# Chunked decay attention ahead of two feed-forward blocks: the work of two neighbouring chunks is issued together

## The chip, the cores and the metric

One Trainium2 chip, one of its cores. The metric is the device time of one execution in microseconds (us); lower is better. Engines are called as the profile calls them: PE (matmuls; PEld is its weight load), DVE (vector), ACT (scalar), POOL (GpSimd), SP (which issues the DMAs).

## What is computed

```
B, H, S, D = 2, 8, 768, 64
intra = (q k^T * decay_mask) v          # inside a block of tokens
inter = (q * lam^(pos+1)) state         # what earlier blocks left behind
out   = intra + inter
state = lam^block * state + (k * lam^(block-1-pos))^T v
x = relu(x w_in)^2 -> s*(.)+b -> w_out   # first feed-forward block
x = rms_norm(x); silu(x w_gate) * (x w_val) -> w_out   # second
```

The reference walks over blocks of 64 tokens, and the kernel over chunks of 128, which is the same recurrence. All is float32.

## The kernel before

There are NG = 12 chunks: 6 per batch row (NCH = 6), each with all 8 heads. Chunks are numbered g = 0 to 11, and c = g % 6 is the place in the batch row. Per chunk and in the names of the trace:

- **sc** (`scores`, L516): 8 matmuls k·q, 64 rows by 128 columns of the array each. DVE multiplies them with the decay into **prob** (L518), two instructions.
- **o** (L558): 8 matmuls v·prob, 128 rows by 64 columns. Then **qs** (L567): 4 matmuls state·qs, 128 by 128, into the same bank. `qs` itself is made by POOL (L530). For c = 0 there is no qs. ACT copies the bank into xq (L578, "the copy").
- **st** (L584): 8 matmuls kdec·v, 128 rows by 64 columns, the new state's part. **kdec** is made by ACT: 8 instructions of 128x64, one for each head (`prepare`, L535). For c = 5 there is neither kdec nor st.
- **state**: POOL scales the state of the chunk before (L546, `prepare_state`), DVE adds st to it (L597, `add_state`).

The order is written out by hand (`manual_schedule`): on every engine instructions run in the order in which the program text issues them. The loop at L624 issues, for chunk g: `prepare(g+1)`, `prepare_state(g)`, `outputs(g)` (o, qs, the copy, st), `add_state(g)`, `scores(g+2)`, then tasks of a table `plan`, which make the operands of the first feed-forward block on ACT and DVE (L143 and L146 split a value into two parts; L123, L129, L135, L140 turn raw words of the weights into numbers), then the loads of chunk g+4. At g = 11 two products of the first feed-forward block (**h**, L295) are issued ahead of `outputs(11)`. After it comes `spread_s`, a tiny matmul (L617) and a copy of its result by DVE (L618), which frees the bank that the third h product needs. Everything behind is one long row of matmuls of the two feed-forward blocks. The diff does not touch it.

Of the kernel before, what the change touches and what calls it, by code (L numbers as in the profile page):

```python
# [7 lines left out]
F32 = mybir.dt.float32  # L8
# [3 lines left out]
AF = mybir.ActivationFunctionType  # L12
# [3 lines left out]
P = 128  # L16
# [6 lines left out]
def attention_moe_moe2_kernel(  # L23
# [15 lines left out]
    nc = tc.nc  # L39
    NG, _, NPAIR, _ = qT.shape  # L40
    H = 2 * NPAIR
    D = P // 2
    B = 2
    NCH = NG // B
# [23 lines left out]
    def bank(i, name):  # L68
        return psum.tile([P, 512], F32, tag=f"b{i}", name=name)
# [5 lines left out]
    def piece(pool, tag, kbs, dtype=F32R):  # L75
        return pool.tile([P, int(kbs * KB)], dtype, tag=tag, name=f"{tag}_{len(made)}_{made.append(tag)}")
# [3 lines left out]
    def at(t, kb, kbs):  # L80
        return t[:, int(kb * KB) : int((kb + kbs) * KB)]
# [4 lines left out]
    def rows(ap):  # L86
        return ap.rearrange("p (k t) -> p k t", k=NK)
# [8 lines left out]
    m_g0 = piece(early, "g", 12, F32)  # L96
# [6 lines left out]
    xq = [rows(t) for t in m_q]  # L103
# [255 lines left out]
    def hquad(i):  # L359
        p, s_ = horder[i]  # L360
        if p < NPLAIN:
            yield from hplain(i)
            return
        ws, xs = w_set(p), ops1[s_]
        b0, b1, b2, b3 = hbanks(i)
        u2 = u2s[i % 2]
        product(b0, ws, xs, A11, B11)
        nc.scalar.activation(m_q1, b0, AF.Copy)
        while late_sq:
            r = late_sq.pop()  # L370
            nc.scalar.activation(r, r, AF.Square)
        yield
        product(b1, ws, xs, S2, T2)
        add(u2, b1, m_q1)
        yield
        r0, r1 = r_place(2 * p, s_), r_place(2 * p + 1, s_)
        u3 = r1[:, HB:BW]
        product(b2, ws, xs, S3, T3)
        add(u3, b2, u2)
        yield  # L380
        product(b3, ws, xs, S1, T1)

        add(u3, b3, u3)
        yield

        product(b0, ws, xs, A12, B21, True)
        nc.scalar.activation(r0[:, 0:HB], b0, AF.Relu)

        product(b2, ws, xs, A22, T4, True)
        add(r1[:, 0:HB], b2, u2)  # L390
        nc.scalar.activation(r1, r1, AF.Relu)

        product(b3, ws, xs, S4, B22, True)
        add(r0[:, HB:BW], b3, u2)
        nc.vector.tensor_scalar(r0[:, HB:BW], r0[:, HB:BW], 0.0, None, op0=ALU.max)
        nc.scalar.activation(r1, r1, AF.Square)
        late_sq.append(r0)
        yield
# [38 lines left out]
    with tc.tile_pool(name="att", bufs=1) as att:  # L437
        qt, kt, kvt = {}, {}, {}
# [14 lines left out]
        def load_chunk(g):  # L453
            if g < NG:
                load_qk(g)
                load_v(g)

        NPRE = 4
# [34 lines left out]
        for hf in range(2):  # L493
            pr = slice(hf * D, (hf + 1) * D)
# [10 lines left out]
        qs, prob, state, o_bank = {}, {}, {}, {}  # L505

        def scores(g):
            if g >= NG:
                return
            pt = att.tile([P, H, P], F32, tag="prob", bufs=3, name=f"prob{g}")  # L510

            sc = [bank(2 * (g % 2) + hf, f"sc{g}_{hf}") for hf in range(2)]
            for i in range(H):
                p, hf = divmod(i, 2)
                pr = slice(hf * D, (hf + 1) * D)
                nc.tensor.matmul(sc[hf][:, p * P : (p + 1) * P], kt[g][pr, p, :], qt[g][pr, p, :], start=True, stop=True)  # L516
            for hf in range(2):
                nc.vector.tensor_tensor(  # L518
                    pt.rearrange("p (a t) i -> p a t i", t=2)[:, :, hf, :],
                    sc[hf].rearrange("p (a i) -> p a i", i=P),  # L520
                    dec.rearrange("p (a t) i -> p a t i", t=2)[:, :, hf, :],
                    op=ALU.mult,
                )
            prob[g] = pt

        def prepare(g):
            c = g % NCH
            if c:
                t = att.tile([P, NPAIR, P], F32, tag="qs", bufs=2, name=f"qs{g}")
                nc.gpsimd.tensor_tensor(t, qt[g], lpow, op=ALU.mult)  # L530
                qs[g] = t
            if c < NCH - 1:
                kd = att.tile([P, H, D], F32, tag="kdec", bufs=2, name=f"kdec{g}")
                for h in range(H):
                    nc.scalar.activation(kd[:, h, :], kvt[g][:, 0, h, :], AF.Copy, scale=dec[:, h, P - 1 : P])  # L535
                qs[g, "kd"] = kd

        def prepare_state(g):
            c = g % NCH
            if c == NCH - 1:  # L540
                return
            sn = att.tile([P, NPAIR, P], F32, tag="state", bufs=2, name=f"state{g}")
            if c == 0:
                nc.gpsimd.memset(sn, 0.0)
            else:
                nc.gpsimd.tensor_tensor(  # L546
                    sn, state[g - 1], lpow[:, :, P - 1 : P].to_broadcast([P, NPAIR, P]), op=ALU.mult
                )
            state[g] = sn

        def outputs(g):
            c = g % NCH
            vn = kvt[g][:, 1]
            last = c == NCH - 1
            o = bank(4 + g % 2, f"o{g}")
            for h in range(H):
                pr = slice(h % 2 * D, (h % 2 + 1) * D)
                nc.tensor.matmul(  # L558
                    o[pr, h // 2 * P : (h // 2 + 1) * P],
                    vn[:, h, :],  # L560
                    prob[g][:, h, :],
                    start=h < 2,
                    stop=c == 0 and h >= H - 2,
                    skip_group_check=True,
                )
            for p in range(NPAIR if c else 0):
                nc.tensor.matmul(  # L567
                    o[:, p * P : (p + 1) * P],
                    state[g - 1][:, p],
                    qs[g][:, p],  # L570
                    start=False,
                    stop=p == NPAIR - 1,
                    skip_group_check=True,
                )
            o_bank[g] = o
            o3 = o.rearrange("p (a i) -> p a i", i=P)
            tok = slice(c * P, (c + 1) * P)
            nc.scalar.activation(xq[g // NCH][:, :, tok], o3, AF.Copy)  # L578
            if not last:
                kd = qs[g, "kd"]  # L580
                st = bank(6 + g % 2, f"st{g}")
                for h in range(H):
                    pr = slice(h % 2 * D, (h % 2 + 1) * D)
                    nc.tensor.matmul(  # L584
                        st[pr, h // 2 * D : (h // 2 + 1) * D], kd[:, h, :], vn[:, h, :], start=True, stop=True
                    )
                return st
            return None

        def add_state(g, st):  # L590
            if st is None:
                return
            st3 = st[:, 0 : NPAIR * D].rearrange("p (a i) -> p a i", i=D)
            sn = state[g]
            for hf in range(2):
                pr = slice(hf * D, (hf + 1) * D)
                nc.vector.tensor_tensor(sn[pr, :, pr], sn[pr, :, pr], st3[pr], op=ALU.add)  # L597

        scores(0)
        scan_lpow()  # L600
        scores(1)
# [9 lines left out]
        w0, w1 = (w_tasks(j, after_w(j)) for j in range(2))  # L611
# [9 lines left out]
            4: [xt["hB11"]], 5: [xt["lB11"], xt["hB21"]], 6: [xt["lB21"]] + w0[0:1], 7: [xt["hB12"]] + w0[1:2],  # L621
            8: [xt["lB12"]] + w0[2:4], 9: [xt["hB22"]] + w0[4:5], 10: [xt["lB22"]] + w1[0:1], 11: [spread_s],
        }
        for g in range(NG):  # L624
            if (g + 1) % NCH == 0 and g + 1 < NG:
                prepare_state(g + 1)
            if g + 1 < NG:
                prepare(g + 1)
            if g % NCH:
                prepare_state(g)  # L630
            if g == NG - 1:

                quad0 = hquad(0)
                next(quad0)
                next(quad0)
                for t in w1[1:]:
                    t()
            st = outputs(g)
            add_state(g, st)
            scores(g + 2)  # L640
            for t in plan.get(g, ()):
                t()
            load_chunk(g + NPRE)
            if g == 4:
                load_w(0, 0)
                load_w(0, 1)
            if g == 8:
                load_w(1, 0)
                load_w(1, 1)
                nc.sync.dma_start(g_col, rms_g.rearrange("(k p) -> p k", p=P))  # L650
                nc.sync.dma_start(row[:, H : H + 1], s.rearrange("(o h) -> o h", o=1))
                nc.sync.dma_start(row[:, H + 1 : H + 2], b.rearrange("(o h) -> o h", o=1))

    late = ctx.enter_context(tc.tile_pool(name="late", bufs=1))
    m_f.update({t: piece(late, t, kbs, F32) for t, kbs in (("u3", 28), ("u4", 15), ("u5", 15), ("u6", 4))})
# [133 lines left out]
    for blk in range(B):  # L789
# [46 lines left out]
        for it in range(by_f):  # L836
# [46 lines left out]
            if it in (3, 4):  # L883
                h = it - 3
# [175 lines left out]
    for i in range(len(order)):  # L1060
        for part, _ in enumerate(quad(i)):
            for t in plan.get((i, part), ()):
                t()
            f = (i + 3) // 2
# [121 lines left out]
```

## Time and profile before

| what | value |
|---|---|
| median of 3 runs | 594.76 us (594.65 to 594.83) |
| span of the profiled execution (first to last instruction) | 592.7 us |
| PE busy | 586.4 us, 99% of the span |
| ACT busy | 321.5 us, 54% |
| DVE busy | 407.8 us, 69% |
| POOL busy | 114.5 us, 19% |
| mean granted TensorE clock | 1.000 of full speed |
| kv load of a chunk, issue to landing | 6.3 us, median of 12 |

The profiled execution is told by its span alone; its own time around the span is not given. The median lies 2.06 us above the span (start and end of the program). Attention takes about the first 56 us of the span, and the rest belongs to the feed-forward blocks. In a timeline row stand the start, the length, the engine, the line, the operation, the tiles and how many instructions were merged; in square brackets stands the idle time of the engine before it and what ended it. Matmuls of float32 leave two records each, so 8 of them read x16.

### The profile page before, as it was taken

To read this page: it belongs to the slowest core of one execution; us is meant where nothing else is said; L and a number is where in the kernel's file an instruction comes from. 1 tells how busy PE (TensorE), PEld (TensorE's weight loads), DVE (VectorE), ACT (ScalarE), POOL (GpSimd) and SP (SyncE) were. 2 spreads that over 40 slices of the span, in tenths; PEclk is the share of its full clock that TensorE was granted. 3 is DMA by queue.
4 is the path that set the end of the run, shared out by engine and by line. 5 is a ranking of instruction groups with operands and counts; after the bars stand their busy time and mean duration, and the time that the engine had idled before them with its cause. 6 is when DMAs were issued, how large, how long until landed. Compare 5 with 4: busy or idle time off the path is not lost.

```text
span 592.7 us, 9212 instructions
## 1 busy us (share of the span) xinstructions
PE 586.4 (99%) x3590; PEld 543.1 (92%) x3590; DVE 407.8 (69%) x654; ACT 321.5 (54%) x572; POOL 114.5 (19%) x118
## 2 busy tenths in 40 slices
PE   9999999999999999999999999999999999999997
PEld 8888999999998888988888999999999998888886
DVE  6587957777777775769947986777777777874200
ACT  5677977777776663646542434444444445763200
POOL 3550032223103232041311002222222200000000
PEclk9999999999999999999999999999999999999999
DMA  8992202223223441221120001221222212320310
GB/s 312 334 350 72 72 1 78 77 72 131 72 72 110 139 143 35 71 69 38 36 72 1 1 2 71 72 72 71 72 72 71 86 58 77 136 72 1 142 38 35
DMA packets 17282, 51.98 MB, mean 88 GB/s; under 512 B 2390, under 2 KB 2390, under 8 KB 17238
## 3 DMA queue, kind: packets, MB, share of 16 engines
q1 hardware_dynamic: 17238, 51.39, 25.4%
q8 instruction: 28, 0.46, 0.3%
q14 instruction: 16, 0.13, 0.1%
HBM read 48.24 MB, written 3.15 MB: 87 GB/s over the span
## 4 chain that ended last, share of the span: by engine, by line
PE 93%; DVE 3%; ACT 2%; issue 1%; DVEq 0%
PE q L295 28%; PE h L295 17%; PE out L1078 17%; PE y L795 15%; PE z L807 8%; PE sc L516 2%; PE o L558 2%; PE o L567 2%; PE st L584 1%; PE warm L481 1%; PE rb L775 0%; DVE r_None L306 0%; PE nps L758 0%; DVE u_None L140 0%; ACT u_None L143 0%
## 5 line engine op out<-in xcount | busy, mean ns | idle before, releaser
L143 ACT ACTIVATE u_None<-u_None 128x768 fp32r<-128x768 f32 (+2 forms) x50 | 42.9, 871 | 55.0 <-DVE u_None L140 48.7
L295 PE MATMUL q<-u0b_None,u_None 128*128 128x384 f32 x360 | 68.4, 336 | 0.0
L295 PEld LDWEIGHTS q<-u0b_None,u_None 128*128 128x128 f32 x360 | 62.8, 188 | 0.6 <-DVE st_None L306 0.3
L146 DVE TENSOR_TENSOR u_None<-u_None,u_None 128x512 fp32r<-128x512 f32 (+1 forms) x66 | 54.1, 845 | 11.0 <-ACT u_None L143 11.0
L218 POOL TENSOR_TENSOR u_None<-u_None 128x256 f32<-128x256 f32 x18 | 19.9, 1103 | 188.6 <-DVE u_None L140 188.6
L295 PE MATMUL q<-xs_None,u_None 128*128 128x384 f32 x288 | 55.3, 334 | 0.0
L123 ACT ACTIVATE u_None<-st_None 128x512 f32<-128x512 f32 x68 | 45.2, 664 | 17.2 <-issue 14.3
L140 DVE CUSTOM_DVE_ANT_0 u_None<-u_None 128x1024 uint16<-128x1024 uint16 x68 | 47.8, 703 | 5.0
L295 PEld LDWEIGHTS q<-xs_None,u_None 128*128 128x128 f32 x288 | 50.4, 188 | 0.0
L129 ACT ACTIVATE u_None<-st_None 128x512 uint32<-128x512 uint16 x68 | 45.3, 666 | 5.1 <-DVE u_None L146 5.1
L306 DVE TENSOR_TENSOR st_None<-q,r_None 128x384 f32<-128x384 f32 x48 | 26.6, 553 | 18.8 <-PE q L295 18.7
L972 ACT ACTIVATE st_None<-r_None 128x384 f32<-128x384 f32 x24 | 12.6, 526 | 47.3 <-DVE r_None L306 47.3
L1078 PE MATMUL out<-u_None,xs_None 128*128 128x512 f32 x144 | 32.8, 389 | 0.0
L1078 PEld LDWEIGHTS out<-u_None,xs_None 128*128 128x128 f32 x144 | 27.0, 188 | 5.6
L1085 DVE COPY st_None<-out 128x512 f32<-128x512 f32 x4 | 2.8, 692 | 40.9 <-PE out L1078 40.9
L135 DVE TENSOR_SCALAR u_None<-u_None 128x512 uint32<-128x512 uint32 x68 | 30.1, 443 | 0.4
L424 POOL TENSOR_TENSOR wsum_None<-wsum_None,u_None 128x512 f32<-128x512 f32 x15 | 20.6, 1377 | 49.0 <-DVE u_None L140 49.0
L295 PE MATMUL q<-u0a_None,u_None 128*128 128x384 f32 x144 | 29.0, 335 | 0.2 <-DVE st_None L306 0.2
L295 PE MATMUL q<-g_None,u_None 128*128 128x384 f32 x144 | 26.9, 334 | 0.0
L295 PEld LDWEIGHTS q<-u0a_None,u_None 128*128 128x128 f32 x144 | 25.3, 188 | 0.5 <-DVE st_None L306 0.5
L1078 PE MATMUL out<-u_None,u0b_None 128*128 128x512 f32 x108 | 25.3, 389 | 0.0
L295 PEld LDWEIGHTS q<-g_None,u_None 128*128 128x128 f32 x144 | 25.1, 188 | 0.0
(202 smaller groups left out, 1310.4 us busy)
## 6 DMA issues: line engine op xcount, KB each, us to landing
st_None<-in_w_dram SPq DMA_DIRECT2D x68, 512.0 KB, 3.3
kv<-in_kv_dram SPq DMA_DIRECT2D x12, 512.0 KB, 6.3
q<-in_qT_dram SPq DMA_DIRECT2D x12, 256.0 KB, 6.8
k<-in_kT_dram SPq DMA_DIRECT2D x12, 256.0 KB, 6.5
out_dram<-st_None SPq DMA_DIRECT2D x8, 256.0 KB, 2.0
out_dram<-u_None SPq DMA_DIRECT2D x4, 256.0 KB, 2.1
row<-in_lam_dram SPq DMA_DIRECT2D x1, 0.0 KB
g_col<-in_rms_g_dram SPq DMA_DIRECT2D x1, 2.0 KB, 3.5
```

Source lines behind the costliest of these rows:

```text
L123: nc.scalar.activation(m, t[:, :, 1].bitcast(F32), AF.Prelu, scale=2.0**-112, alpha=-(2.0**32))
L129: nc.scalar.activation(to.bitcast(U32), low, AF.Copy, scale=2.0**-13)
L135: nc.vector.tensor_scalar(m, m, 3, None, op0=ALU.logical_shift_left)
L140: nc.vector.tensor_tensor(m, m, t.bitcast(U32), op=ALU.add)
L143: nc.scalar.activation(to, src, AF.Copy)
L146: nc.vector.tensor_tensor(to, src, hi.bitcast(F32), op=ALU.subtract)
L295: nc.tensor.matmul(ps, ws[:, wi, wop * KC + kt * P : wop * KC + (kt + 1) * P], xs[xop][:, xi, kt, :], start=n == 0 and not more, stop=n == ...
L306: nc.vector.tensor_tensor(to, ps, more, op=ALU.add)
L424: nc.gpsimd.tensor_tensor(wsum, wsum, m, op=ALU.add)
L795: nc.tensor.matmul(acc[d], wt[:, wi, d * P : (d + 1) * P], gt[:, gi, 0:BT], start=it == 0 and pi == 0, stop=it == NF1 - 1 and pi == 2,)
L807: nc.tensor.matmul(acc2[d // 2][:, d % 2 * BX : (d % 2 + 1) * BX], wt[:, wi, d * P : (d + 1) * P], gt[:, gi, BT:BW], start=it == 0 and pi ...
L1078: nc.tensor.matmul(ps, rows_[:, ai], w_out[f][:, wi, :], start=first and pi == 0, stop=last and pi == 2)
```

## The change

The loop goes over pairs of chunks. `outputs` is split into `states` (the st matmuls), `within` (the o matmuls) and `before` (the qs matmuls and the copy). For a pair g, g+1 it issues: st of both, o of both, `prepare_state(g)`, `add_state(g)`, qs and copy of g, `prepare_state(g+1)`, the tasks of g, `add_state(g+1)`, qs and copy of g+1, `prepare` of g+2 and g+3, sc of g+2 and g+3, the tasks of g+1, the loads of chunks g+4 and g+5. In the first pair o stands ahead of st. prob gets a fourth buffer, and the state moves to three places in a buffer that is otherwise unused at that time.

```diff
-            pt = att.tile([P, H, P], F32, tag="prob", bufs=3, name=f"prob{g}")
+            pt = att.tile([P, H, P], F32, tag="prob", bufs=4, name=f"prob{g}")
...
-            sn = att.tile([P, NPAIR, P], F32, tag="state", bufs=2, name=f"state{g}")
+            sn = at(m_g0, 2 * (g % 3), 2).rearrange("p (a i) -> p a i", i=P)
...
-        for g in range(NG):
-            if (g + 1) % NCH == 0 and g + 1 < NG:
-                prepare_state(g + 1)
-            if g + 1 < NG:
-                prepare(g + 1)
-            if g % NCH:
-                prepare_state(g)
...
-            st = outputs(g)
-            add_state(g, st)
-            scores(g + 2)
...
-            load_chunk(g + NPRE)
...
+        prepare(1)
+        for g in range(0, NG, 2):
+            if g:
+                st = [states(g + i) for i in range(2)]
+            within(g)
+            within(g + 1)
+            if not g:
+                st = [states(g + i) for i in range(2)]
+            if g % NCH:
+                prepare_state(g)
+            add_state(g, st[0])
+            before(g)
+            prepare_state(g + 1)
+            tasks(g)
+            if g + 2 == NG:
+                quad0 = hquad(0)
+                next(quad0)
+                next(quad0)
+                for t in w1[1:]:
+                    t()
+            add_state(g + 1, st[1])
+            before(g + 1)
+            for i in range(2, 4):
+                if g + i < NG:
+                    if (g + i) % NCH == 0:
+                        prepare_state(g + i)
+                    prepare(g + i)
+            scores(g + 2)
+            scores(g + 3)
+            tasks(g + 1)
+            for i in range(NPRE, NPRE + 2):
+                load_chunk(g + i)
+            fetch_more(g)
```

On PE, from the end of sc of chunk 3 on (the number behind a name's letters is the chunk; the last number is a buffer's). Before:

```order
L516 MATMUL sc3_1_281<-q3_111,k3_113 128x128
L558 MATMUL o2_311<-prob2_222,kv2_109 64x128 x8
L567 MATMUL o2_311<-qs2_241,state1_252 128x128 x4
L584 MATMUL st2_325<-kv2_109,kdec2_243 64x64 x8
L516 MATMUL sc4_0_337<-q4_235,k4_237 128x128
```

And now:

```order
L516 MATMUL sc3_1_284<-q3_111,k3_113 128x128
L558 MATMUL st2_307<-kv2_109,kdec2_249 64x64 x8
L558 MATMUL st3_316<-kv3_115,kdec3_260 64x64 x8
L568 MATMUL o2_325<-prob2_269,kv2_109 64x128 x8
L568 MATMUL o3_334<-prob3_282,kv3_115 64x128 x8
L581 MATMUL o2_325<-qs2_247,g_7_None_73 128x128 x4
L581 MATMUL o3_334<-qs3_258,g_7_None_73 128x128 x4
L516 MATMUL sc4_0_373<-q4_295,k4_297 128x128
```

The st matmuls moved from the end of a chunk's work to the front of the pair's, and each kind stands in one row for two chunks.

On ACT, where kdec is made and the outputs are copied, chunks 1 to 4. Before:

```order
L535 ACTIVATE kdec1_192<-kv1_103,dec_135 128x64 x8
L578 ACTIVATE xq0_5_None_71<-o0_201 128x4x128
L535 ACTIVATE kdec2_243<-kv2_109,dec_135 128x64 x8
L578 ACTIVATE xq0_5_None_71<-o1_254 128x4x128
L535 ACTIVATE kdec3_300<-kv3_115,dec_135 128x64 x8
L578 ACTIVATE xq0_5_None_71<-o2_311 128x4x128
```

And now:

```order
L535 ACTIVATE kdec1_191<-kv1_103,dec_135 128x64 x8
L590 ACTIVATE xq0_5_None_71<-o0_200 128x4x128
L590 ACTIVATE xq0_5_None_71<-o1_209 128x4x128
L535 ACTIVATE kdec2_249<-kv2_109,dec_135 128x64 x8
L535 ACTIVATE kdec3_260<-kv3_115,dec_135 128x64 x8
L590 ACTIVATE xq0_5_None_71<-o2_325 128x4x128
```

kdec of chunk g+1 stood ahead of the copy of chunk g; now kdec of both chunks of a pair stands behind both copies of the pair before.

Further on ACT, chunks 8 to 10 (L129 and L143 to u2 are tasks for the weights of the first h products), now:

```order
L590 ACTIVATE xq1_6_None_72<-o8_646 128x4x128
L129 ACTIVATE u1_2_None_68<-st0_11_None_77 128x512
L143 ACTIVATE u2_3_None_69<-u1_2_None_68 128x1024
L590 ACTIVATE xq1_6_None_72<-o9_655 128x4x128
L535 ACTIVATE kdec10_687<-kv10_620,dec_135 128x64 x8
```

Before, the copy of o9 stood behind kdec10; the two tasks already stood ahead of it.

## Rows read from the trace of the kernel before

**Rows 1.** Span and granted clock of the core; then the page's busy times.

```profile
core 0: 592.7 us, clock 1.000
...
PE 586.4 (99%) x3590; PEld 543.1 (92%) x3590; DVE 407.8 (69%) x654; ACT 321.5 (54%) x572; POOL 114.5 (19%) x118
```

**Rows 2.** Timeline of PE, one regular chunk: start, length, line, tiles, count.

```profile
15.18 1.16 PE L516 MATMUL sc<-q,k 64*128 64x128 f32 x16
16.27 1.09 PE L558 MATMUL o<-prob,kv 128*64 128x128 f32 x16
17.30 1.16 PE L567 MATMUL o<-qs,state 128*128 128x128 f32 x8
18.38 0.69 PE L584 MATMUL st<-kv,kdec 128*64 128x64 f32 x16
19.00 1.16 PE L516 MATMUL sc<-q,k 64*128 64x128 f32 x16
```

**Rows 3.** Timeline of PE, chunk 6, which has no qs.

```profile
30.93 1.09 PE L558 MATMUL o<-prob,kv 128*64 128x128 f32 x16
31.86 0.64 PE L584 MATMUL st<-kv,kdec 128*64 128x64 f32 x16
32.42 1.16 PE L516 MATMUL sc<-q,k 64*128 64x128 f32 x16
```

**Rows 4.** Timeline of PEld at two changes of tile shape.

```profile
17.29 0.97 PEld L567 LDWEIGHTS o<-qs,state 128*128 128x128 f32 x8 [0.17 <-issue]
...
53.10 0.85 PEld L558 LDWEIGHTS o<-prob,kv 128*64 128x64 f32 x16 [0.25 <-issue]
```

**Rows 5.** Timeline of ACT: kdec, copies, and the tasks of the plan.

```profile
12.84 2.01 ACT L535 ACTIVATE kdec<-kv,dec 128x64 f32<-128x64 f32 x8
14.75 0.58 ACT L578 ACTIVATE xq_None<-o 128x512 f32<-128x512 f32 x1
...
18.49 0.60 ACT L578 ACTIVATE xq_None<-o 128x512 f32<-128x512 f32 x1 [1.15 <-PE o L567]
...
26.62 0.84 ACT L143 ACTIVATE u0b_None<-xq_None 128x768 fp32r<-128x768 f32 x1
...
40.81 0.67 ACT L129 ACTIVATE u_None<-st_None 128x512 uint32<-128x512 uint16 x1
45.45 1.06 ACT L143 ACTIVATE u_None<-u_None 128x1024 fp32r<-128x1024 f32 x1 [3.98 <-DVE u_None L140]
46.42 2.01 ACT L535 ACTIVATE kdec<-kv,dec 128x64 f32<-128x64 f32 x8
```

**Rows 6.** Timeline of PE where that kdec is used, chunk 10.

```profile
47.39 1.42 PE L584 MATMUL st<-kv,kdec 128*64 128x64 f32 x16
48.73 2.35 PE L295 MATMUL h<-u0b_None,u_None 128*128 128x384 f32 x12
```

**Rows 7.** Timeline of PE: the first o, and the third h product.

```profile
9.78 1.19 PE L558 MATMUL o<-prob,kv 128*64 128x128 f32 x16
...
55.84 2.38 PE L295 MATMUL h<-u0b_None,u_None 128*128 128x384 f32 x12 [0.25 <-DVE params L618]
```

**Rows 8.** Timeline of DVE, first two chunks: prob of chunk 1, then the state.

```profile
11.27 0.68 DVE L518 TENSOR_TENSOR prob<-sc,dec 128x512 f32<-128x512 f32 x1
11.86 0.84 DVE L597 TENSOR_TENSOR state<-state,st 64x256 f32<-64x256 f32 x2
```

**Rows 9.** DVE's L140 at two places, and POOL beside the first.

```profile
43.88 1.54 DVE L140 CUSTOM_DVE_ANT_0 u_None<-u_None 128x1024 uint16<-128x1024 uint16 x1
...
51.29 0.69 DVE L140 CUSTOM_DVE_ANT_0 u_None<-u_None 128x1024 uint16<-128x1024 uint16 x1
...
43.42 1.45 POOL L530 TENSOR_TENSOR qs<-q,lpow 128x512 f32<-128x512 f32 x1 [1.10 <-PE o L567]
```

**Rows 10.** ACT's copy of o10, and the end of the chain of tasks on DVE.

```profile
49.54 0.58 ACT L578 ACTIVATE xq_None<-o 128x512 f32<-128x512 f32 x1
...
55.63 0.16 DVE L618 COPY params<-params 128x2 f32<-128x2 f32 x1
```

More of the change, by code (lines that the diff above doesn't have):

```diff
@@ L549, in prepare_state, with states, within @@
             state[g] = sn
-        def outputs(g):
-            c = g % NCH
+        def states(g):
+            if g % NCH == NCH - 1:
+                return None
+            vn, kd = kvt[g][:, 1], qs[g, "kd"]
+            st = bank(6 + g % 2, f"st{g}")
+            for h in range(H):
+                pr = slice(h % 2 * D, (h % 2 + 1) * D)
+                nc.tensor.matmul(
+                    st[pr, h // 2 * D : (h // 2 + 1) * D], kd[:, h, :], vn[:, h, :], start=True, stop=True
+                )
+            return st
+        def within(g):
             vn = kvt[g][:, 1]
-            last = c == NCH - 1
             o = bank(4 + g % 2, f"o{g}")
@@ L562, in outputs, with before @@
                     start=h < 2,
-                    stop=c == 0 and h >= H - 2,
+                    stop=g % NCH == 0 and h >= H - 2,
                     skip_group_check=True,
                 )
+            o_bank[g] = o
+        def before(g):
+            c, o = g % NCH, o_bank[g]
             for p in range(NPAIR if c else 0):
@@ L574, in outputs @@
                 )
-            o_bank[g] = o
-            o3 = o.rearrange("p (a i) -> p a i", i=P)
             tok = slice(c * P, (c + 1) * P)
[L578 to L588, printed above, removed]
+            nc.scalar.activation(xq[g // NCH][:, :, tok], o.rearrange("p (a i) -> p a i", i=P), AF.Copy)
         def add_state(g, st):
@@ L623, in attention_moe_moe2_kernel, with tasks, fetch_more @@
         }
-        for g in range(NG):
-            if (g + 1) % NCH == 0 and g + 1 < NG:
-                prepare_state(g + 1)
-            if g + 1 < NG:
-                prepare(g + 1)
-            if g % NCH:
-                prepare_state(g)
[L631 to L637, printed above, removed]
-            st = outputs(g)
-            add_state(g, st)
-            scores(g + 2)
+        def tasks(g):
             for t in plan.get(g, ()):
                 t()
-            load_chunk(g + NPRE)
+        def fetch_more(g):
             if g == 4:
```

## The prediction

> **What bounds the kernel now.** I read the page first: PE is busy 586.4 of the 592.7 us of the span, and ACT half of it [rows 1]. So PE's own time is the limit, and a change pays only where it shortens that time and does not make PE wait. Next I read PE's timeline through attention. A regular chunk is sc 1.09, o 1.03, qs 1.08, st 0.62, from start to start, 3.82 us in all, with no gap [rows 2]. The next thing to see is that part of this is paid for changing kinds. In chunk 6, which has no qs between o and st, the two take 1.49 instead of 1.03 + 0.62 = 1.65 [rows 3]: one change of tile shape less, 0.16 us less. PEld's timeline shows the same thing from the other side, a gap of 0.17 to 0.25 us that nothing releases at each change [rows 4]. I take 0.20 us for a change, between 0.16 and 0.25. Last I read ACT, because the order shows that its instructions move. There kdec takes 1.91 us to the next start, and 0.10 of an instruction's length overlaps the next one, so a copy costs 0.48 [rows 5].
>
> The place that decides my forecast is one that went wrong already before the change. From 41.5 to 45.45 ACT stood still for 3.98 us in front of a task (L143) that waited for DVE; kdec of chunk 10 stood behind it and began only at 46.42 [rows 5]. On PE st of chunk 10 then took 1.42 instead of 0.69, and h began at 48.73, which is 0.30 after kdec's end at 48.43 [rows 6]. So ACT takes its instructions in order, and PE waits in st for a late kdec, with everything behind it. 0.20 of the 0.30 is the change of shape, so 0.10 is the handover, which I use for every handover below.
>
> **What the change takes away.** Counted from the first o to the third h product (9.78 to 55.84 us [rows 7]) PE changes shape 42 times before. With the change it does so 18 times, because st and o have one shape and stand together, and qs of chunk 10, h and qs of chunk 11 do too. That is 24 changes less: 24 x 0.20 = **4.8 us less** (3.8 to 6.0). A pair that never waits would take 7.64 - 5 x 0.20 = 6.64 us.
>
> **What it adds.** kdec of a pair now stands on ACT behind both copies of the pair before it, and the last copy waits for the last qs on PE. But st of the new pair is what PE wants right after sc. Let S be the start of sc of a pair. The copy starts 0.11 after PE has left qs, as at 18.38 and 18.49 [rows 2, 5]. Then the first o can start at 0.11 + 0.48 + 2 x 1.91 + 0.10 + 0.10 = S + 4.61. Without the wait it would be sc twice, 2 x 1.09 - 0.20 = 1.98, and st twice, 2 x 0.42, so S + 2.82. PE waits 1.79 us. Then o twice, 2 x 1.03 - 0.20 = 1.86, and qs twice, 2 x 1.08 - 0.20 = 1.96. **A pair lasts 8.43 us where it lasted 7.64.** The five changes saved are there, and the wait eats more.
>
> The whole path on PE, pair by pair:
> - Pair 0, 1: o of chunk 1 waits for its prob, which ends at 11.27 + 0.68 = 11.95 [rows 8]; before, sc of chunk 2 stood in that time. Handover 0.10, seven of eight heads 0.73, st of chunk 0 0.42, handover 0.10, `add_state` 0.84 [rows 8], handover 0.10, qs 1.08: sc of chunk 2 starts at 15.3.
> - Pair 2, 3: 8.43, to 23.8.
> - Pair 4, 5: chunk 5 has no kdec. 0.11 + 0.48 + 1.91 + 0.20 = 2.70, o 1.86, qs 1.96: 6.52, to 30.3.
> - Pair 6, 7: the task hB11 (L143, 0.74) stands between the two copies of chunks 4 and 5. The first copy starts at S - 0.97 and ends at S - 0.49, the task ends at S + 0.25, the second copy at S + 0.73. kdec twice and handover 4.02, o 1.86, and only one qs, 1.08: 7.69, to 38.0.
> - Pair 8, 9: the copy of chunk 6 needs no qs and is early, so the two word tasks between the copies (2 x 0.57) are over in time: 8.43, to 46.4.
> - Pair 10, 11: after the copy of chunk 8 (S - 0.49) come L129 (0.57), L140 on DVE, L143 (0.97), the copy of chunk 9 (0.48), then one kdec with its handover 2.11, o 1.86, qs of chunk 10 without a change 0.88. L140 takes 0.69 us alone and took 1.54 while POOL made a qs [rows 9]; in the new order POOL makes two qs just there, so I take 1.54. Sum 7.92, and h starts at 54.3 (53.5 with 0.69). It was 48.73.
> - The third h product needs the copy L618, behind the tasks of ACT and DVE that begin with the copy of chunk 10: 49.54 to 55.84 took 6.30 [rows 7, 10]. PE itself needs 7.11 - 1.03 = 6.08, as o of chunk 11 is done earlier. So 0.11 + 6.30 after h: 60.7.
>
> 60.7 against 55.84 is **+4.9 us**: 4.8 gained, 9.7 given to waits. Behind this point the same matmuls follow in the same order, at 99% [rows 1], and the loads of weights come no later against PE, so I carry the 4.9 to the end. The sum stands on one profiled execution with a span of 592.7 [rows 1]; the span becomes 597.6, and the median, 2.06 us above the span, 594.76 + 4.9 = **599.7 us**.
>
> What I cost at nothing: the state's chain (POOL scales, DVE adds, 1.9 us for a chunk) is needed only one pair later for the first chunk, and after o twice for the second; if it were late, qs would wait. The added DVE distance between prob and its o is covered by the kdec wait itself. The loads of chunks g + 4 and g + 5 are let go later: the kv buffer for chunk 6 is free when o of chunk 2 is done, near 15.3 + 5.5 = 20.8, and kdec wants chunk 6 near 30.3 + 0.7 = 31.0. That is 10 us, and a kv load landed in 6.3 us (the table of the profile before). The state's new place costs nothing to anyone.
>
> The Trainium skill, TensorEngine Tiling (Array Packing), PSUM Bottleneck, says that after a speedup by tiling the copies out of PSUM may become the limit. Here the rows weigh otherwise. DVE reads four prob and two `add_state` pairs for a pair of chunks, 4 x 0.68 + 2 x 0.84 = 4.4 us [rows 8], and ACT's copies take 0.96, both below 6.64. By that rule alone nothing would bind and the sum would be -4.8; by the rows it is +4.9, since kdec and not a copy is late.
>
> **Unknown sizes.** The 1.54 may be 0.69: 4.0 instead of 4.9. A change of 0.25 or 0.16 instead of 0.20 moves some nine pieces that are on the path by 0.05 or 0.04: -0.45 or +0.36. Handovers may be 0.2 instead of 0.1, two or three for a pair: up to +1.3. So the forecast's own range is +3.3 to +6.7, 598.0 to 601.5.
>
> **Rivals.**
> - *Only the changes of shape count (faster).* If kdec is ready when sc ends, because the copies are early or ACT runs kdec quicker, PE never waits and the time is 594.76 - 4.8 = 590.0. For it: 24 changes really go. Against it: 3.8 us of kdec do not fit beside 2 us of sc, and the order has them behind the copies. The point that decides: a pair of chunks breaks even with 7.64 when one kdec takes 1.91 - 0.79 / 2 = 1.52 us. Chance 6%. The Trainium skill, TensorEngine Tiling (Array Packing), Key Properties, says that changing the tiling mode drains the TensorE; by that rule alone this rival would be right, and the trace's 0.16 agrees on the drain.
> - *The two cancel.* If the first pair and the last one cost less than written (5.5 and 7.9 us), and pairs break even, the time is within 0.2% (1.2 us), which is about what a measurement of this kernel can tell from no change: 594.8. For it: two of six pairs have one kdec or none late. Against it: pair 2, 3, pair 6, 7 and pair 8, 9 each lose 0.8 us or more. Chance 5%.
> - *The waits also slow PE's clock (slower still).* The granted clock is 1.000, the level of 2.4 GHz, with PE at 99% [rows 1]; now PE stands still for 1.8 us in each of several pairs. At 1.2 GHz one pair would need 5.6 to the first o, then 3.72 and 3.92: 13.2 instead of 8.43, so +4.8 and 604.5 for one pair. Against it: the st at 47.39 held a wait of 0.73 us, and 12 h records after it took 2.35 us as against 2.38 later [rows 6, 7]. Chance 4%. The Trainium skill, TensorE: Matmul & The Clock Gate, Part 1, says that the clock is throttled unless activity releases it; no trace here shows how short a wait is harmless.
>
> **How the numbers follow.** The forecast, waits for kdec beyond the gain, has 85%, and gives 599.7. Faster 6%, same 5%, slower 89% (85 and 4). The range leaves out the faster rival, most of "cancel" and the clock, some 15%, and is a little wider than the forecast's own: 597.5 to 602.5.
>
> **What would show it.** In the profile after: PE's st of the second chunk of pairs 2, 3, 6, 7 and 8, 9 some 1.8 us long, or idle there with ACT kdec as releaser; sc, sc, st, o of a pair from S to S + 8.4; h at 54 and its third product near 60.7; L140 near 46.5 long beside POOL. It is wrong if sc of chunk 4 starts before 22.5 (15.3 + 7.2), or if ACT's kdec of chunk 2 starts before the copy of chunk 1, or if PE busy falls by 5 us and the span with it.

## The result, and the profile after

| | before | with the change |
|---|---|---|
| median | 594.77 us | 600.62 us (600.47 to 601.08, 4 runs) |
| ratio | | 1.0104, 95% interval 1.0092 to 1.0116 |
| span of the profiled execution | 592.7 us | 598.5 us |

The kernel is 1% slower, 5.85 us; forecast were 599.7 (597.5 to 602.5) and slower. The page after shows where not to look:

```profile
PE 589.6 (99%) x3590; PEld 546.9 (91%) x3590; DVE 409.4 (68%) x654; ACT 321.9 (54%) x572; POOL 114.5 (19%) x118
```

PE's busy time did not fall by 4.8 us, it rose by 3.2 [rows 1]: the st matmuls trickle in, one for each kdec instruction every 0.24 us, and their records are 0.22 to 0.27 us long, so the wait between them counts as busy. So the waits are read from starts. PE's timeline after, the starts of all pairs from chunk 2 on (st and o of two chunks read x32, or x31 beside a stray row of one; `g_None` is the state's new place):

```profile
15.72 2.06 PE L516 MATMUL sc<-q,k 64*128 64x128 f32 x32
17.70 2.87 PE L558 MATMUL st<-kv,kdec 128*64 128x64 f32 x31
...
20.47 1.91 PE L568 MATMUL o<-prob,kv 128*64 128x128 f32 x31
22.31 2.05 PE L581 MATMUL o<-qs,g_None 128*128 128x128 f32 x16
24.29 2.06 PE L516 MATMUL sc<-q,k 64*128 64x128 f32 x32
...
31.02 2.06 PE L516 MATMUL sc<-q,k 64*128 64x128 f32 x32
...
39.02 2.06 PE L516 MATMUL sc<-q,k 64*128 64x128 f32 x32
...
47.59 2.06 PE L516 MATMUL sc<-q,k 64*128 64x128 f32 x32
50.55 1.94 PE L558 MATMUL st<-kv,kdec 128*64 128x64 f32 x15 [0.90 <-ACT kdec L535]
...
55.14 2.35 PE L295 MATMUL h<-u0b_None,u_None 128*128 128x384 f32 x12
...
61.70 2.35 PE L295 MATMUL h<-u0b_None,u_None 128*128 128x384 f32 x12 [0.92 <-DVE params L620]
```

st of chunks 2 and 3 takes 2.77 us to the next group, where the same 16 matmuls without a wait take 0.98 (the kernel with kdec early, below). All the other kinds go at the pace the sum used. The third h product starts at 61.70 instead of 55.84 [rows 7], 5.86 us later, and the span is 5.8 us longer: behind it nothing came back and nothing was added. ACT's timeline after, ahead of pair 2, 3 and of the last pair:

```profile
15.82 0.60 ACT L590 ACTIVATE xq_None<-o 128x512 f32<-128x512 f32 x1 [3.43 <-PE o L581]
16.32 3.93 ACT L535 ACTIVATE kdec<-kv,dec 128x64 f32<-128x64 f32 x16
...
46.80 0.60 ACT L590 ACTIVATE xq_None<-o 128x512 f32<-128x512 f32 x1 [1.88 <-PE o L581]
47.30 0.66 ACT L129 ACTIVATE u_None<-st_None 128x512 uint32<-128x512 uint16 x1
48.72 1.06 ACT L143 ACTIVATE u_None<-u_None 128x1024 fp32r<-128x1024 f32 x1 [0.76 <-DVE u_None L140]
49.68 0.58 ACT L590 ACTIVATE xq_None<-o 128x512 f32<-128x512 f32 x1
50.16 2.01 ACT L535 ACTIVATE kdec<-kv,dec 128x64 f32<-128x64 f32 x8
```

ACT stands idle for 3.43 us in front of a copy that waits for qs, with kdec of chunks 2 and 3 queued behind it; then PE waits for kdec, which ends at 20.25, and o follows at 20.47. At the end of the stage the two tasks and the copy of chunk 9 stand between, and kdec of chunk 10 starts only at 50.16, 2.57 us after sc.

### The profile page after: what moved, and what is told of

It is laid out like the page before. It is cut to its first block, busy times and chain, and to the rows that moved or that the text cites. A ratio compares the mean times of both kernels' runs of the same rounds, so it can differ in the third digit from the quotient of the medians.

```text
span 598.5 us, 9209 instructions
## 1 busy us (share of the span) xinstructions
PE 589.6 (99%) x3590; PEld 546.9 (91%) x3590; DVE 409.4 (68%) x654; ACT 321.9 (54%) x572; POOL 114.5 (19%) x118
## 4 chain that ended last, share of the span: by engine, by line
PE 92%; DVE 3%; ACT 3%; issue 1%; DVEq 0%; ACTq 0%
PE q L295 28%; PE out L1101 16%; PE h L295 16%; PE y L818 15%; PE z L830 8%; PE st L558 2%; PE sc L516 2%; PE o L568 2%; PE o L581 2%; PE warm L481 1%; PE rb L798 0%; DVE u_None L140 0%; DVE r_None L306 0%; PE nps L781 0%; ACT u_None L123 0%
## 5 line engine op out<-in xcount | busy, mean ns | idle before, releaser
L143 ACT ACTIVATE u_None<-u_None 128x768 fp32r<-128x768 f32 (+2 forms) x50 | 42.8, 870 | 51.8 <-DVE u_None L140 45.5
L140 DVE CUSTOM_DVE_ANT_0 u_None<-u_None 128x1024 uint16<-128x1024 uint16 x68 | 47.0, 691 | 6.0 <-ACT u_None L129 1.2
L129 ACT ACTIVATE u_None<-st_None 128x512 uint32<-128x512 uint16 x68 | 45.2, 665 | 5.1 <-DVE u_None L146 5.1
L135 DVE TENSOR_SCALAR u_None<-u_None 128x512 uint32<-128x512 uint32 x68 | 31.0, 455 | 2.0 <-ACT u_None L123 1.6
L295 PE MATMUL h<-u0b_None,u_None 128*128 128x384 f32 x126 | 24.3, 337 | 0.9 <-DVE params L620 0.9
```

Source lines behind the costliest of these rows:

```text
L129: nc.scalar.activation(to.bitcast(U32), low, AF.Copy, scale=2.0**-13)
L135: nc.vector.tensor_scalar(m, m, 3, None, op0=ALU.logical_shift_left)
L140: nc.vector.tensor_tensor(m, m, t.bitcast(U32), op=ALU.add)
L143: nc.scalar.activation(to, src, AF.Copy)
L295: nc.tensor.matmul(ps, ws[:, wi, wop * KC + kt * P : wop * KC + (kt + 1) * P], xs[xop][:, xi, kt, :], start=n == 0 and not more, stop=n == ...
```

## The experiments

Theory A: kdec stands on ACT behind the copies, st stands on PE at the front of a pair, and the two together make the wait. Rival B: the pairs as such cost, by prob, the state or the loads, and kdec only hides it. The fourth prob buffer and the state's new place stand in every version of the change below.

**kdec early.** `prepare` is split, and its kdec part is issued as soon as st has freed the buffers:

```diff
...
+            for i in range(2, 4):
+                if g + i < NG:
+                    prepare_k(g + i)
             if g % NCH:
                 prepare_state(g)
             add_state(g, st[0])
             before(g)
```

> The change with one thing undone: kdec of the next pair is issued on ACT ahead of both copies of this pair (st and o have just freed its buffers). Theory A (PE waits in st because kdec stands behind the copies): st of a pair no longer waits, a pair lasts 6.6 to 6.9 us instead of 8.57, h starts near 48.8 instead of 55.1, and the time falls by 6 to 7 us, to 594.3 (593.5 to 595). Rival B (the pairs themselves cost: prob, the state's chain or the loads are late and kdec only hides it): another wait takes the place, a pair stays at 8 us or more and the time at 599 or above.

Measured 596.79 us, ratio 1.0026 (1.0012 to 1.0039). PE's timeline of this kernel:

```profile
15.72 2.06 PE L516 MATMUL sc<-q,k 64*128 64x128 f32 x32
17.70 1.15 PE L561 MATMUL st<-kv,kdec 128*64 128x64 f32 x32
18.68 1.92 PE L571 MATMUL o<-prob,kv 128*64 128x128 f32 x32
20.53 2.05 PE L584 MATMUL o<-qs,g_None 128*128 128x128 f32 x16
22.51 2.06 PE L516 MATMUL sc<-q,k 64*128 64x128 f32 x32
...
29.25 2.06 PE L516 MATMUL sc<-q,k 64*128 64x128 f32 x32
...
35.77 2.06 PE L516 MATMUL sc<-q,k 64*128 64x128 f32 x32
...
38.74 2.29 PE L571 MATMUL o<-prob,kv 128*64 128x128 f32 x32
...
43.05 2.06 PE L516 MATMUL sc<-q,k 64*128 64x128 f32 x32
...
47.45 4.07 PE L571 MATMUL o<-prob,kv 128*64 128x128 f32 x32 [1.73 <-DVE prob L518]
51.45 1.16 PE L584 MATMUL o<-qs,g_None 128*128 128x128 f32 x8
52.36 2.33 PE L295 MATMUL h<-u0b_None,u_None 128*128 128x384 f32 x12
```

In pair 2, 3 theory A holds: 8.57 became 6.79, near the 6.64 of a pair that never waits. Pair 8, 9 went from 8.57 to 7.28 only, as o took 2.22 instead of 1.85 to the next group, and pair 4, 5 stayed (6.74 after 6.73). The time fell by 3.8 us and not by 6 to 7. The last pair took 9.31 from sc to h instead of 7.55. There rival B has its part: o of chunk 10 waits 1.73 us for prob, and DVE is why.

```profile
42.75 1.27 DVE L135 TENSOR_SCALAR u_None<-u_None 128x512 uint32<-128x512 uint32 x1
44.16 1.54 DVE L140 CUSTOM_DVE_ANT_0 u_None<-u_None 128x1024 uint16<-128x1024 uint16 x1
45.73 0.85 DVE L602 TENSOR_TENSOR g_None<-g_None,st 64x256 f32<-64x256 f32 x2
46.61 2.48 DVE L518 TENSOR_TENSOR prob<-sc,dec 128x512 f32<-128x512 f32 x4
```

The words of the first weights stand ahead of prob of chunk 10, and both DVE instructions are stretched (0.42 and 0.69 us elsewhere in the trace). The late kdec had covered that. And o behind the wait takes twice its time (4.07 instead of 1.92). The windows of this execution (their length, then the busy time of PE, PEld, DVE, ACT and POOL, then the granted clock and what the DMAs did) say why:

```profile
46.00:48.00 2.00, 0.45 (x4) 0.24 (x4) 1.96 (x5) 2.00 (x3) 1.84 (x2) 0.96 0.15 11
48.00:50.00 2.00, 2.00 (x20) 2.00 (x22) 2.00 (x4) 0.01 (x1) 0.00 (x0) 0.50 0.00 0
50.00:52.00 2.00, 2.00 (x19) 1.78 (x15) 1.96 (x4) 0.00 (x0) 0.00 (x0) 0.68 0.00 0
```

PE was busy for 0.45 of 2 us, and then the clock was granted at half, 1.2 GHz, until some time after 50. That loses some 0.04 x 2 + 0.50 x 2 + 0.32 x 2 = 1.7 us, an estimate from these rows. Half of this kernel's six executions had a mean clock of 0.996 and took 597.4 to 597.6, the others 595.7 to 596.2: at the full clock, too, it is slower than the kernel before (595.04 in this round).

**kdec late in the old order.** The kernel before, with kdec of chunk g+1 moved behind the copy of chunk g:

```diff
...
             st = outputs(g)
+            if g + 1 < NG:
+                prepare_k(g + 1)
```

> The kernel before with kdec of chunk g+1 moved behind the copy of chunk g, and nothing else. Theory A says that the place behind the copy hurts only together with st at the front: here st of chunk g+1 comes 3.82 us after st of chunk g and kdec is done 0.11 + 0.48 + 1.91 + 0.20 = 2.70 us after it, so nothing waits in the regular chunks; 594.8 to 595.6, a little only at chunk 10, where tasks stand in between. Rival B2 (kdec behind the copy costs wherever st stands): about 0.8 us for each of nine chunks, 600 or more.

Measured 595.39 us, ratio 1.0002 (0.9993 to 1.0012). In the regular chunks nothing waits, though kdec now starts right behind the copy; st keeps its 0.69, and sc of two neighbouring chunks stand 3.82 apart (15.09 and 18.91) as before:

```profile
14.58 0.60 ACT L581 ACTIVATE xq_None<-o 128x512 f32<-128x512 f32 x1 [1.16 <-PE o L570]
15.07 2.01 ACT L538 ACTIVATE kdec<-kv,dec 128x64 f32<-128x64 f32 x8
18.29 0.69 PE L587 MATMUL st<-kv,kdec 128*64 128x64 f32 x16
```

So kdec behind the copy is harmless as long as sc, o and qs of the next chunk stand ahead of the st that wants it; at chunk 10, with the tasks between, st took 1.90 instead of 1.42. It takes both halves of the change, as theory A has it.

**st behind o.** All pairs with `within` ahead of `states`, as the first has it.

> The change with st of both chunks behind o of both in every pair, as the first pair has it. kdec stays behind the copies. Theory A: o twice (1.66 us) moves into the wait for kdec, so each pair with two kdec gains 1.1 to 1.7 us, up to what the state (DVE's add behind st, ahead of qs) gives back; 597.0 (596 to 598.5). Rival B (not kdec but the pairs as such): no gain, 600.6.

Measured 601.03 us, ratio 1.0103 (1.0086 to 1.012): a miss. Three pairs did gain from sc to sc (2, 3: 7.66 us instead of 8.57; 6, 7: 7.45 instead of 8.00; 8, 9: 8.09 instead of 8.57), but pair 4, 5 lost (7.47 instead of 6.73): o right behind sc waits for DVE's four prob, and o twice took 2.46 there instead of 1.85. The last pair lost too: sc of chunk 10 to h took 8.30 instead of 7.55, with PE standing in front of o of chunk 10 (PE, then DVE):

```profile
49.70 2.72 PE L568 MATMUL o<-prob,kv 128*64 128x128 f32 x31 [2.10 <-ACT xq_None L590]
...
48.91 2.48 DVE L518 TENSOR_TENSOR prob<-sc,dec 128x512 f32<-128x512 f32 x4
```

The profile names ACT's copy of o9 as what ended the wait. But by the program that copy empties the bank of o of chunk 11; the bank of o of chunk 10 had been copied out by 45.4. What o of chunk 10 needs is its prob, which begins on DVE only at 48.91, behind the two word tasks, as in kdec early; its halves end at 49.60 and 50.20, and the first two heads of o start at 49.70 and 50.25. Three of the four executions had a mean clock of 0.996 or 0.997 and took 600.5 to 601.5; the profiled one had the full clock and took 599.26, which is above the expected range as well. I had costed the matmuls that move into the wait, and not the prob that they need.

**kdec in half the instructions.**

```diff
-                for h in range(H):
-                    nc.scalar.activation(kd[:, h, :], kvt[g][:, 0, h, :], AF.Copy, scale=dec[:, h, P - 1 : P])
+                for h in range(0, H, 2):
+                    nc.scalar.activation(kd[:, h : h + 2, :], kvt[g][:, 0, h : h + 2, :], AF.Copy, scale=dec[:, h, P - 1 : P])
```

> The change with kdec in 4 ACT instructions of 128x128 for a chunk instead of 8 of 128x64; the second head of each two gets the decay of the first, which leaves out part of the computation. One kdec takes about 1.15 us instead of 1.91, which is under the 1.52 us at which a pair breaks even with the kernel before. Theory A: 2 x 0.75 us less for each pair with two kdec and 0.75 for those with one, as far as the wait reaches: 594.6 (594 to 596). Rival B: 600 or more.

Measured 596.88 us, ratio 1.0033 (1.0024 to 1.0043): 3.7 us less than the change, its order untouched, and above the expected 594 to 596. Pair 2, 3 lasts 7.09 (15.71 to 22.80) instead of 8.57. So the dose matters, which rival B cannot explain. The point of breaking even was right for a pair (7.09 is below 7.64), and wrong for the whole, as the first and last pairs carry waits of another kind: sc of chunk 10 (43.32) to h (51.70) took 8.38 instead of 7.55, with kdec of chunk 10 behind a word task that waited for DVE.

```profile
47.90 1.21 PE L558 MATMUL st<-kv,kdec 128*64 128x64 f32 x16 [2.52 <-ACT kdec L535]
```

**The price of a change of shape.** kdec early, but with qs of the first chunk between the two o:

```diff
...
             within(g)
-            within(g + 1)
+            if g % NCH == 0:
+                within(g + 1)
...
             before(g)
+            if g % NCH:
+                within(g + 1)
```

> kdec early, but in pairs 2, 3, 4, 5, 8, 9 and 10, 11 qs of the first chunk stands between the two o, as in the kernel before: two more changes of tile shape in a pair, same matmuls. If a change costs 0.16 to 0.25 us, the pairs 2, 3 and 4, 5 last 0.3 to 0.5 us longer than with kdec early alone (6.79 and 6.74 us), less what the later second o saves by waiting less for its prob (at most 0.3 in pair 4, 5). If a change costs nothing on the path, they last the same 6.8.

Measured 596.07 us, ratio 1.0031 (1.0021 to 1.0041). Pair 2, 3 of this kernel:

```profile
15.71 2.06 PE L516 MATMUL sc<-q,k 64*128 64x128 f32 x32
17.70 1.15 PE L561 MATMUL st<-kv,kdec 128*64 128x64 f32 x32
18.68 1.09 PE L571 MATMUL o<-prob,kv 128*64 128x128 f32 x16
19.70 1.16 PE L584 MATMUL o<-qs,g_None 128*128 128x128 f32 x8
20.78 1.09 PE L571 MATMUL o<-prob,kv 128*64 128x128 f32 x16
21.81 1.16 PE L584 MATMUL o<-qs,g_None 128*128 128x128 f32 x8
22.90 2.06 PE L516 MATMUL sc<-q,k 64*128 64x128 f32 x32
```

It lasts 7.19 us with two changes more, against 6.79: 0.20 us for each. In pairs 4, 5 and 8, 9 the two cost next to nothing (6.75 against 6.74, 7.27 against 7.28), since the later o no longer waits for its prob. The whole kernel was not slower than kdec early either (596.07 and 596.79; at the full clock 595.5 to 596.1 and 595.7 to 596.2). The gain is real, and it counts only where nothing else is late.

**Repairs, one behind the other.** First the words go behind prob of chunks 10 and 11, then the tiny matmul of `spread_s` gets another bank, one that sc used, then the first two chunks go back to nearly the old order, last the words go between the two prob:

```diff
...
-            8: [xt["lB12"]] + w0[2:4], 9: [xt["hB22"]] + w0[4:5],
+            8: [xt["lB12"]], 9: w0[2:4] + w0[4:5] + [xt["hB22"]],
...
-            pps = bank(6, "params2")
+            pps = bank(3, "params2")
```

> kdec early, and the word tasks of the first weights (L129, L135, L140, L143) moved from the tasks of chunk 8 to those of chunk 9, which is behind prob of chunks 10 and 11 on DVE and behind kdec and both copies on ACT. Theory C (with kdec early the last pair waits because DVE's prob stands behind that chain of words: 9.31 us from sc of chunk 10 to h): o of chunk 10 no longer waits for prob, PE's long wait near 46 us goes and with it the half clock behind it; sc of chunk 10 to h takes 6.5 to 7.5 us, some of which the first h product gives back by waiting for its words; 595.0 (594 to 596). Rival D (the words are late whatever stands ahead of them): the wait moves to h unchanged, 596.5 to 597.

595.79 us, ratio 1.0014 (1.0005 to 1.0024), no half clock in the stage. sc of chunk 10 to h took 6.42 instead of 9.31. The first h product gave 1.0 of it back, waiting for DVE's words (3.20 to the next product instead of 2.17), and the third waited 1.38 instead of 0.94. Theory C holds for the wait in front of o and for the clock; the rest of the wait moved on, as rival D has it. Against the kernel before of its own round (594.82) this version is 0.97 us slower; the executions of kdec early at the full clock were 0.7 to 1.2 slower than theirs. So the repair took away the half clock and little else.

> The same, and the tiny matmul of spread_s writes to a bank that sc used, so the third h product no longer waits for DVE's copy L620. Expected where the copy is what it waits for: the wait of 0.93 us ahead of the third h product goes, 0.9 to 1.6 us less than the kernel without this, 593.8 (593 to 595), which would be below the kernel before. Where the second weights' words are what counts, the wait moves to the fifth product and nothing is gained.

594.53 us, ratio 0.9993 (0.9983 to 1.0002): the wait ahead of the third h product is gone, the time equal to the kernel before.

> Control: the kernel before with the tiny matmul of spread_s on another bank, and nothing else. Only the wait of 0.25 us ahead of the third h product can go: 594.5 to 594.8, the same within what can be told. If it gains 0.9 us or more, the gain of the bank has nothing to do with the pairs.

594.16 us, ratio 0.9988 (0.9979 to 0.9998), 0.37 below the repaired pairs of the same round: so far pairing gains nothing over the old order with the same bank. Beside the last two kernels once more:

> The control once more, beside the two: the kernel before with the other bank. 594.2, the same as before (594.0 to 594.6).

594.74 us, ratio 0.9997 (0.9988 to 1.0006). Both medians of the control lie just outside what was expected of them, one below and one above; they are 0.58 us apart, so a gain of that size can't be told here. The bank alone is worth at most that in the old order, where o of chunk 11 stands ahead.

> As the version with kdec early, words behind prob and the other bank, but chunks 0 and 1 in nearly the old order: o and st of chunk 0, sc of chunk 2, o and st of chunk 1, qs of chunk 1, sc of chunk 3; pairs from chunk 2 on. Theory E (pairing pays for the changes saved with waits where nothing else stands between dependent steps, 2.15 us of them in the first pair): sc of chunk 2 covers the wait for prob of chunk 1, st of chunk 2 starts 1.2 to 1.4 us earlier against the first o, two changes more; 593.3 (592.8 to 594), faster than the kernel before by 0.2 to 0.3%. Rival: the wait comes back later at the loads or the words, and the time stays at 594.5.

```diff
+        within(0)
+        add_state(0, states(0))
+        before(0)
...
+        scores(2)
+        within(1)
+        add_state(1, states(1))
...
+        before(1)
...
+        scores(3)
...
+        for g in range(2, NG, 2):
```

593.47 us, ratio 0.9981 (0.9972 to 0.999): 1.06 us less than without it (measured in another round), 1.27 less than the control of the same round (594.74), which is about twice what the control's two medians differ by, and 0.2% below the kernel before. The fourth prob buffer and the state's new place are in it, so they do not make the loss. sc of chunk 2 now covers the wait for prob of chunk 1:

```profile
10.99 1.16 PE L516 MATMUL sc<-q,k 64*128 64x128 f32 x16
12.08 1.09 PE L571 MATMUL o<-prob,kv 128*64 128x128 f32 x16
13.01 0.63 PE L561 MATMUL st<-kv,kdec 128*64 128x64 f32 x16
13.57 1.16 PE L584 MATMUL o<-qs,g_None 128*128 128x128 f32 x8
14.66 1.16 PE L516 MATMUL sc<-q,k 64*128 64x128 f32 x16
```

> The same, with the words of the first weights between prob of chunk 10 and prob of chunk 11 on DVE instead of behind both. The first h product no longer waits 1.3 us for its words, o of chunk 11 waits up to 1 us more for its prob: between 0.5 us less and nothing, 592.8 to 593.5.

594.71 us, ratio 0.9998 (0.9989 to 1.0006): a miss. o of chunk 11 waited 1.56 us for its prob, and in the profiled execution the clock went to half behind it. That is not all: the ten executions with a mean clock of 0.999 or 1.000 have a median of 594.5. The wait was moved to a worse place.

## Why the prediction was right, point by point

| step, from sc to sc | forecast | measured |
|---|---|---|
| first pair, to sc of chunk 2 | 15.3 | 15.72 |
| pair 2, 3 | 8.43 | 8.57 |
| pair 4, 5 | 6.52 | 6.73 |
| pair 6, 7 | 7.69 | 8.00 |
| pair 8, 9 | 8.43 | 8.57 |
| chunk 10, sc to h | 7.92 | 7.55 |
| h to the third h product | 6.41 | 6.56 |
| third h product later than before by | 4.9 | 5.86 |

- **The mechanism** stands as forecast: kdec early takes the wait for kdec out of the pairs, fewer kdec instructions shorten it, and kdec late in the old order does nothing to the regular chunks. The size of the wait was met too: the change and kdec early both start pair 2, 3 at 15.72, and its qs at 22.31 and 20.53, 1.78 us apart, where the forecast has 1.79.
- **The gain**, 24 changes at 0.20 us: the price was measured at 0.20 in the one pair of three where nothing else was late. Where two groups of a kind became one, the rows give the same: sc twice takes 1.98 instead of 2 x 1.09, o twice 1.85 instead of 2 x 1.03, qs twice 1.98 instead of 2 x 1.08. PEld does not show it at each change, as the prediction reads it: in the kernel before its gap is 0.17 ahead of qs and 0.07 to 0.12 ahead of sc, o and st. The Trainium skill, TensorEngine Tiling (Array Packing), Key Properties, says that changing the tiling mode drains the TensorE; the trace agrees, and gives the drain this size here.
- **The small terms** were short by 0.14 to 0.31 us for each pair up to 8, 9, and 0.4 in the first. From the end of kdec to the row of o it took 0.22 in pair 2, 3, with the last head of st in it, and 0.21 to 0.23 in the others; the sum has a handover of 0.10 there. In the first pair the handover from st to the state's add was too short: the add began at 13.66, where the sum has 13.30; it ended at 14.51, and qs began at 14.66. With the last two steps (0.37 too high, 0.15 too low) they are the 1.0 us by which the sum was low.
- **L140** was mis-sized. I took 1.54 us for it, as two qs of POOL would run beside it; it took 0.69, though POOL's two qs ran from 46.85 on: the first ended at 48.13, only 0.14 after L140 began (the last section has the rule that the traces show). That term came out 0.85 too high and hid part of the others. This was luck: with 0.69 in it, the prediction's own sum is 4.0 and its time 598.8, 1.8 below the measured one. DVE's timeline after:

```profile
47.99 0.69 DVE L140 CUSTOM_DVE_ANT_0 u_None<-u_None 128x1024 uint16<-128x1024 uint16 x1 [1.18 <-ACT u_None L129]
```

POOL's timeline of the same execution, the first of the two qs:

```profile
46.85 1.28 POOL L530 TENSOR_TENSOR qs<-q,lpow 128x512 f32<-128x512 f32 x1 [0.32 <-PE o L581]
```

- **The rival "only the changes count"** was wrong in its number too: with kdec on time the time did not come to 590.0 but to 596.8, and after three repairs to 593.5. Pairing also takes away the work that stood between dependent steps: prob and o, words and h, copy and third product. My sum had these only where they were late beside kdec.
- **The rival on the clock** did not come true here: 0.999 in the mean, with no half clock within the stage. It came true in some executions of other versions; a mean clock of 0.996 or 0.997 stands in three of six with kdec early, three of four with st behind o, three of ten with kdec in half the instructions, four of ten with qs between, and two of twelve with the words between.

## What to carry to other kernels

Grouping matmuls of one tile shape saved 0.20 us for each change here where nothing else was late, but it brings the producer of the group's first operand to the front: look at what stands ahead of that producer on its own in-order engine, and issue it as soon as its buffer is free. A long wait can cover others, so after taking it out, look for the next one before counting the gain. Where PE has nothing independent left, keep the old interleaving, as at the first two chunks here.

## What was not expected of the hardware

A stand of PE of about 2 us is not always free of a further price: with PE busy for 0.45 of the 2 us from 46 to 48, the clock was granted at 0.50 from 48 to 50 and at 0.68 from 50 to 52, and some 1.7 us were lost. Half of the executions of this one kernel had the lower mean clock, and so it has two times, 1.6 us apart. Nor does each such stand cost: with kdec in half the instructions PE was busy for 0.10 of 2 us, and the clock stayed at 1.00.

```profile
46.00:48.00 2.00, 0.10 (x2) 0.11 (x4) 1.95 (x4) 1.99 (x4) 2.00 (x2) 1.00 0.28 52
48.00:50.00 2.00, 2.00 (x36) 1.71 (x38) 2.00 (x5) 1.45 (x4) 0.12 (x1) 1.00 0.03 8
```

With st behind o it was busy for 0.29 of the 2 us from 48 to 50, at 1.00 then and behind it. What decides was not tried. The Trainium skill, TensorE: Matmul & The Clock Gate, Part 1, says that activity releases the throttle; the trace with kdec early agrees: PE was busy all through the rows from 48 to 52, and from 52 on the clock was at 1.00 again.

DVE's L135 took 1.27 us and L140 1.54 in the kernel with kdec early, against 0.42 and 0.69 elsewhere, each time beside a POOL instruction; but L140 also took 0.69 beside one. The traces show what goes with it: the end of the POOL instruction that was already running. An L140 that begins beside one ends 0.55 to 0.56 us behind it, and an L135 0.28 to 0.29, in the attention stage of every trace here that has the case. With kdec early POOL's qs ended at 45.16 and L140 at 45.70; in the kernel before at 44.87 and 45.42; with the change at 48.13 and 48.69. So a short overlap costs nothing, and a long one nearly all of POOL's rest. No run moved a POOL instruction to test this.
